# Dealing parts of a weight gradient to fifteen of the sixteen DMA engines, and moving late stores to another queue

## The chip, the cores and the metric

The kernel runs on one core of a Trainium2 chip. The time is what the device needs for one execution, in microseconds; the median of three runs before the change is 733.99 us (733.68 to 734.82).

A core has a matrix engine (PE, with its weight loads PEld), a vector engine (DVE), a scalar engine (ACT), a general one (POOL) and a sequencer for transfers (SP). Transfers between HBM and on-chip memory are issued from the queues of SP, ACT and POOL and carried by 16 DMA engines. In the profile SP's transfers are queue q1, ACT's q10 and Pool's q0.

## The reference

One decode step: forward and backward of `x + attention(layernorm(x)) + mlp(layernorm(x))`, in bf16. One token, model width 640, 32 heads of 128 with caches of 8192 keys and values per head.

```
xn   = layernorm(x)
q    = xn @ wq                               # 640 x 4096
p    = softmax(q k^T * 128**-0.5)            # per head, 8192 keys
o    = p v
out  = x + o @ wo + mlp(xn)                  # wo: 4096 x 640; w1, w3, w2: 640 x 1728 and back
returns out and the gradients of x, k_cache, v_cache, wq, wo, w1, w3, w2
```

Caches and their gradients are 64 MiB each: 128 MiB is read and 128 MiB written for them. wq, wo and their gradients are 5 MiB each. For one token the gradients are outer products: that of V is p times the gradient of o, that of K is the gradient of the scores times q, that of wq is xn times the gradient of q.

## The kernel before

**Per head.** Each head's K and V (2 MiB each) are loaded by SP into three K and two V buffers, up to three heads ahead (`load_k`, `load_v`). `product` multiplies on DVE (line 365) and lets PE sum with an identity matrix (line 367); `row_max`, `exps` and `probs` make the softmax; `attend` and `dscores` make o and the gradient of q on PE. `outer` writes the gradient of V and of K into one of four buffers `ot`, most of it on DVE (line 387), sixteen of 64 rows on ACT (line 380). `store_made` sends a full `ot`, 2 MiB, from ACT's queue (line 403); the last two heads send halves from SP's queue (line 392).

**Per group.** Four heads make a group `g`, eight a batch `b`. A group has 512 columns of wq and a tile `wo_g` of wo. `prep_steps(g + 1)` makes q for the next group from `wq` (line 263), and transposes `wo_g` on PE (line 253) for the gradient of o; these steps run in `gap()`, between the work of a head. `load_wo(g + 1)` is issued from Pool's queue in the second head of a group (line 146), into one of two buffers. `finish_steps(g)` overwrites `wo_g` and the group's wq columns in place with their gradients on ACT (lines 313 and 323) and stores `wo_g` from Pool's queue (line 319).

**wq.** There are two buffers of a batch each, 128 partitions by 5 columns (`ci`) by 1024 elements. Row `5 p + ci` of wq lies in partition `p`, column `ci`: a column of a batch is 128 pieces of 2 KiB, 256 KiB. Batches 0 and 1 are loaded whole by SP. For batches 0 and 1 the gradient goes out from Pool's queue column by column: the first when the batch's second group is finished, then two after each second half of an `outer` (line 396). Batches 2 and 3 are loaded, also by column, into the same buffers from Pool's queue, at places of the third and fourth head of a batch (`WQ_AT`, line 652). A load waits for the store of the column that it overwrites.

**Late stores.** Three stores are put off until head 29: the gradient of wq of batch 2 (1.25 MiB), that of wo of group 6 and that of wq of group 6 (0.625 MiB each). They go out from ACT's queue in one row (`late`, line 697). The last group's wq gradient, `dwq_t`, goes out from ACT's queue at the very end (line 735).

**Order.** Every engine's instructions run in the order in which the program writes them. An instruction that waits holds up all that stands behind it on its engine, and a queue's transfers are issued in the same way.

Of the kernel before, what the change touches and what calls it, by code (L numbers as in the profile page):

```python
# [9 lines left out]
BF16 = mybir.dt.bfloat16  # L10
# [6 lines left out]
P = 128  # L17
# [4 lines left out]
def kernel(  # L22
# [22 lines left out]
    nc = tc.nc  # L45
    H = A_k_cache.shape[1]
    SK = A_k_cache.shape[2]
    DH = A_k_cache.shape[3]
# [3 lines left out]
    NC = D // P  # L52
# [6 lines left out]
    GW = 8  # L59
# [2 lines left out]
    NB = NF + 1  # L62
    ACT_J = 8
    TAIL = 2
    assert H % GW == 0 and GW % GH == 0 and 0 < REST < P and P % GH == 0
    scale = float(DH) ** -0.5

    consts = ctx.enter_context(tc.tile_pool(name="consts", bufs=1))
# [18 lines left out]
    wq_v = A_wq.rearrange("(p ci) n -> p ci n", ci=NC)  # L87
    dwq_v = out_4.rearrange("(p ci) n -> p ci n", ci=NC)
# [9 lines left out]
    with tc.manual_schedule(engines=ORDERED):  # L98
# [22 lines left out]
        grp = {}  # L121
        late = []

        def store(dst, src, later=False):
            if later:
                late.append((dst, src))
            else:
                nc.scalar.dma_start(dst, src)


        wq_bufs = [consts.tile([P, NC, GW * DH], BF16, name=f"wq_{i}") for i in range(2)]

        def load_wq(b, columns=None, queue=None):
            wq_g = wq_bufs[b % 2]
            cols = slice(b * GW * DH, (b + 1) * GW * DH)
            if columns is None:
                nc.sync.dma_start(wq_g[:], wq_v[:, :, cols])
            for ci in columns or ():
                queue.dma_start(wq_g[:, ci, :], wq_v[:, ci, cols])
            for g in range(b * HB, (b + 1) * HB):  # L140
                c0 = (g - b * HB) * GH * DH
                grp.setdefault(g, dict(wq_all=wq_g, wq=wq_g[:, :, c0:c0 + GH * DH]))
# [148 lines left out]
        def on_cols(g):  # L291
            on = small.tile([P, GH], F32, name="on")
            nc.scalar.copy(on[:], grp[g]["on_ps"])
            on_bf = small.tile([P, GH], BF16, name="on_bf")
            nc.scalar.copy(on_bf[:], on[:])
            return on, on_bf
# [8 lines left out]
        def finish_steps(g):  # L305
            G_ = grp[g]
            wo_g = G_["wo"]
            on, on_bf = on_cols(g)
            behind_o.append((g, on_bf))
            yield  # L310
            assert not behind_o
            for r in range(GH):
                nc.scalar.activation(wo_g[:, r, :], g_bc_bf[:], ACTF.Copy, scale=on[:, r:r + 1])
                if r == 1:
                    yield
            if g == NG - 2:
                store(dwo_v[g], wo_g[:], True)
            else:
                nc.gpsimd.dma_start(dwo_v[g], wo_g[:])
            yield  # L320
            b, k = divmod(g, HB)
            for ci in range(NC):
                nc.scalar.activation(G_["wq"][:, ci, :], G_["dqbc"][:].rearrange("p h d -> p (h d)"),
                                     ACTF.Copy, scale=xn_col[:, ci:ci + 1])
            if g < NG - HB and k == HB - 1:
                cols = slice(b * GW * DH, (b + 1) * GW * DH)
                if g == NG - HB - 1:
                    store(dwq_v[:, :, cols], G_["wq_all"][:], True)
                else:
                    columns.extend((dwq_v[:, ci, cols], G_["wq_all"][:, ci, :]) for ci in range(NC))  # L330
                    nc.gpsimd.dma_start(*columns.pop(0))
            if g >= NG - HB:
                store(dwq_v[:, :, g * GH * DH:(g + 1) * GH * DH], G_["wq"], True)
            grp.pop(g)
# [7 lines left out]
        def new_head(h):  # L342
            st = Head()
            st.h = h
            st.g, st.hh = divmod(h, GH)
            st.G = grp[st.g]
            st.K, st.V = kv_tiles.pop(h)
            hs[h] = st
            return st

        def product(st, which, half):
            if which == "S":
                st.q = st.G["qs"][:, st.hh, :]
# [12 lines left out]
            for i in range(DHH // RUN):  # L366
                nc.tensor.matmul(ps[:], lhsT=ident_bf[:], rhs=T[:, :, RUN * i:RUN * (i + 1)],  # L367
                                 start=(half == 0 and i == 0), stop=(half == 1 and i == DHH // RUN - 1))

        def outer(st, vec, w2, wf, dst, h, half):  # L370
            outer_v(st, vec, w2, dst, h, half, outer_s(st, vec, wf, half))
# [12 lines left out]
        def outer_v(st, vec, w2, dst, h, half, j1):  # L384
            j0 = half * JH
            n = j1 - j0
            nc.vector.tensor_tensor(st.ot[:, j0:j1],  # L387
                                    vec.rearrange("p (a b) -> p a b", b=2).unsqueeze(1).to_broadcast([P, n, DH // 2, 2]),
                                    w2[:, j0:j1, :].unsqueeze(2).to_broadcast([P, n, DH // 2, 2]), ALU.mult)
            rows = st.ot[:].rearrange("p j a b -> p j (a b)")  # L390
            if h >= H - TAIL:
                nc.sync.dma_start(dst[h][:, j0:j0 + JH, :], rows[:, j0:j0 + JH, :])
            elif half:
                made.append((dst[h], rows))
                for _ in range(2 if len(columns) > 2 else len(columns)):
                    nc.gpsimd.dma_start(*columns.pop(0))

        columns = []
        made = []

        def store_made():
            while made:
                nc.scalar.dma_start(*made.pop(0))
# [195 lines left out]
        for b in range(NB):  # L599
            rows, src = (P, w2t[:, b, :]) if b < NF else (REST, w2r)  # L600
# [37 lines left out]
        def gap():  # L638
            if steps and next(steps[0], "end") == "end":
                steps.pop(0)  # L640
# [8 lines left out]
        exps(first)  # L649
        product(first, "DP", 1)  # L650
        prev = None
        WQ_AT = {(2, 1): ((0,), nc.gpsimd), (3, 0): ((1,), nc.gpsimd), (3, 1): ((2,), nc.gpsimd), (3, 2): ((3, 4), nc.gpsimd)}

        def wq_columns(h, part):
            b, r = divmod(h, GW)
            if 0 < b < H // GW - 1 and (r, part) in WQ_AT:
                load_wq(b + 1, *WQ_AT[r, part])

        for h in range(H - 1):
            n = new_head(h + 1) if h + 1 < H else None  # L660
            c = hs.pop(h)
            g, hh = divmod(h, GH)
            if n:
                product(n, "S", 0)
            probs(c)
            outer(c, c.do, c.P2, c.Pf, dvc, h, 0)
            if prev:
                keep_dq(prev)
            gap()
            row_dots(c)  # L670
            attend(c)
            turn_wq(c)
            if n:
                product(n, "S", 1)
            outer(c, c.do, c.P2, c.Pf, dvc, h, 1)
            if h + 2 < H:
                load_v(h + 2)
            wq_columns(h, 0)
            if hh == 1 and 0 < g < NG - 1:
                load_wo(g + 1, nc.gpsimd)  # L680
            gap()
            dscores(c)
            store_made()
            outer(c, c.q, c.U2, c.Uf, dkc, h, 0)
            keep_wq(c)
            if n:
                row_max(n)
                product(n, "DP", 0)
            outer(c, c.q, c.U2, c.Uf, dkc, h, 1)
            if h == 0:  # L690
                load_k(4)
            elif 1 < h < H - 3:
                load_k(h + 3)
            wq_columns(h, 1)
            wq_columns(h, 2)
            if h == H - 3:
                for dst, src in late:
                    store(dst, src)
            gap()
            if n:  # L700
                exps(n)
                store_made()
                product(n, "DP", 1)
            weights(c)
            gap()
            if hh == 1 and g + 1 < NG:
                steps.append(prep_steps(g + 1))
            if hh == 2:
                gap()
            prev = c  # L710
# [86 lines left out]
```

## Time and profile before

| | |
|---|---|
| median of three runs | 733.99 us |
| the profiled execution | 733.73 us, its span 732.0 us |
| DVE busy | 630.8 us (86%) |
| PE busy | 550.5 us (75%) |
| ACT busy | 462.1 us (63%) |
| moved by DMA | 303.71 MB, mean 415 GB/s |
| SP's queue (q1) | 153.84 MB, 50.2% of 16 engines' span |
| ACT's queue (q10) | 129.11 MB, 41.6% |
| Pool's queue (q0) | 19.75 MB, 6.5% |

Times inside an execution are microseconds from the start of its span. The page's slices cut the span into 40 equal parts. A window row gives a stretch, its length, the busy time of PE, PEld, DVE, ACT and POOL with the number of instructions, the clock granted to PE, the DMA share (the mean busy share of the 16 DMA engines) and GB/s. A row of the timeline gives start, duration, engine, line and operation; in brackets stands how long the engine had been idle and what ended that. "ACTq" and "SPq" are the queues' own issuing instructions.

### The profile page before, as it was taken

How to read it: one execution, taken by the hardware profiler on the slowest of the kernel's cores; microseconds unless marked ns; L12 is line 12 of the kernel's file. 1: busy time of each engine (PE TensorE's matmuls, PEld its weight loads, DVE VectorE, ACT ScalarE, POOL GpSimd, SP SyncE). 2: the span in 40 equal slices, each digit the busy share in tenths (PEclk: the TensorE clock that was granted, in tenths of full speed). 3: DMA queues.
4: the chain of work that ended last, by engine and by line, in shares of the span. 5: the costliest groups of instructions: out<-in, count | busy, mean ns of one | idle time of the engine just before them, and what ended most of it. 6: DMA issues, size and time to landing. Idle time of an engine off the chain costs nothing.

```text
span 732.0 us, 15729 instructions
## 1 busy us (share of the span) xinstructions
PE 550.5 (75%) x6499; PEld 327.6 (45%) x6513; DVE 630.8 (86%) x720; ACT 462.1 (63%) x1391; POOL 21.9 (3%) x46
## 2 busy tenths in 40 slices
PE   5778887788787648876878674887787878887482
PEld 4654444444444425443444432444444445444151
DVE  4789899999999777988899975999889988999774
ACT  2175656786678464784678743777567846777172
POOL 0010000000001100000000200000000000000000
PEclk9697788868888877887876876877887667777685
DMA  9999999999999999999999999999999999999887
GB/s 360 405 420 427 428 428 424 406 429 428 427 431 427 429 426 428 427 428 429 429 428 428 427 429 429 403 428 428 428 429 422 427 424 428 407 428 421 340 328 281
DMA packets 27687, 303.71 MB, mean 415 GB/s; under 512 B 3084, under 2 KB 4430, under 8 KB 9950
## 3 DMA queue, kind: packets, MB, share of 16 engines
q1 hardware_dynamic: 12914, 153.84, 50.2%
q10 hardware_dynamic: 10764, 129.11, 41.6%
q0 software_dynamic: 3936, 19.75, 6.5%
q8 instruction: 51, 0.84, 0.4%
q14 instruction: 22, 0.18, 0.1%
HBM read 151.34 MB, written 151.34 MB: 414 GB/s over the span
## 4 chain that ended last, share of the span: by engine, by line
DMA 41%; issue 19%; DVE 18%; PE 17%; ACT 4%; SPq 0%; POOL 0%; DVEq 0%; POOLq 0%; ACTq 0%
DMA Kt<-in_A_k_cache_dram 19%; DMA out_dram<-wo_g 9%; DVE T L365 9%; DMA wo_g<-in_A_wo_dram 8%; DVE ot L387 5%; PE psS L367 5%; DMA Vt<-in_A_v_cache_dram 3%; PE psDP L367 3%; ACT ot L380 2%; PE ob L434 2%; PE ob L456 2%; DMA dbc<-in_B_w_dram 2%; DVE DP_sb L441 1%; PE dx_ps L551 1%; PE up_ps L526 1%
## 5 line engine op out<-in xcount | busy, mean ns | idle before, releaser
L367 PEld LDWEIGHTS <-ident_bf 128*128 128x128 bf16 x1024 | 121.1, 120 | 237.2 <-issue 183.0
L367 PE MATMUL psDP<-T,ident_bf 128*128 128x512 bf16 x512 | 178.5, 511 | 58.6 <-DVE T L365 58.6
L365 DVE TENSOR_TENSOR T<-Kt,qs_g 128x4096 bf16<-128x4096 bf16 x64 | 146.5, 2290 | 37.1 <-DMA Kt<-in_A_k_cache_dram 35.3
L380 ACT ACTIVATE ot<-qs_g,Uf 128x128 bf16<-128x128 bf16 x496 | 151.4, 389 | 31.6 <-DVE Uf L454 31.6
L367 PE MATMUL psS<-T,ident_bf 128*128 128x512 bf16 x512 | 149.4, 445 | 27.5 <-DVE T L365 27.4
L380 ACT ACTIVATE ot<-do_g,Pf 128x128 bf16<-128x128 bf16 x504 | 154.0, 389 | 1.0
L365 DVE TENSOR_TENSOR T<-Vt,do_g 128x4096 bf16<-128x4096 bf16 x64 | 146.1, 2283 | 5.0 <-ACT do_g L284 2.8
L387 DVE TENSOR_TENSOR ot<-do_g,P 128x3072 bf16<-128x3072 bf16 (+1 forms) x64 | 112.9, 1763 | 1.1
L387 DVE TENSOR_TENSOR ot<-qs_g,U 128x3072 bf16<-128x3072 bf16 (+1 forms) x64 | 113.2, 1768 | 0.0
L456 PEld LDWEIGHTS <-Kt 128*128 128x128 bf16 x2048 | 58.2, 99 | 11.0 <-issue 7.7
L456 PE MATMUL ob<-U,Kt 128*128 128x1 bf16 x2048 | 57.5, 164 | 1.6 <-DVE U L449 1.5
L434 PEld LDWEIGHTS <-Vt 128*128 128x128 bf16 x2048 | 56.7, 97 | 0.0
L434 PE MATMUL ob<-P,Vt 128*128 128x1 bf16 x2048 | 56.0, 163 | 0.0
L475 ACT ACTIVATE dq_diag<-ident_bf,odq 128x128 bf16<-128x128 bf16 x32 | 12.9, 402 | 67.6 <-DVE odq L471 53.8
L428 ACT ACTIVATE Pf<-E,rZ 128x16 f32<-128x16 f32 x32 | 9.8, 305 | 57.6 <-DVE rZ L424 57.6
L258 ACT COPY woT<-ps_t 128x512 bf16<-128x512 bf16 x40 | 23.1, 579 | 33.3 <-PE ps_t L253 33.2
L253 PE MATMUL ps_t<-ident_bf,wo_g 128*128 128x128 bf16 x160 | 17.8, 242 | 32.0 <-DMA wo_g<-in_A_wo_dram 22.3
L253 PEld LDWEIGHTS <-wo_g 128*128 128x128 bf16 x160 | 13.8, 109 | 42.7 <-DMA wo_g<-in_A_wo_dram 23.8
L407 DVE TENSOR_REDUCE S_sb<-psS 128x64 f32<-128x512 f32 x32 | 22.0, 687 | 5.3 <-PE psS L367 5.3
L419 ACT ACTIVATE E<-S_sb,negM 128x64 f32<-128x64 f32 x32 | 11.1, 346 | 24.0 <-DVE negM L416 23.6
L445 PEld LDWEIGHTS sm<-rdot,ones_fc 128*128 128x128 f32 x64 | 11.2, 197 | 29.7 <-DVE junk L444 26.6
L445 PE MATMUL sm<-rdot,ones_fc 128*128 128x1 f32 x64 | 11.1, 242 | 17.7 <-DVE junk L444 17.6
(158 smaller groups left out, 504.9 us busy)
## 6 DMA issues: line engine op xcount, KB each, us to landing
out_dram<-ot ACTq DMA_DIRECT2D x60, 2048.0 KB, 26.7
Kt<-in_A_k_cache_dram SPq DMA_DIRECT2D x32, 2048.0 KB, 28.1
Vt<-in_A_v_cache_dram SPq DMA_DIRECT2D x32, 2048.0 KB, 22.1
out_dram<-ot SPq DMA_DIRECT2D x8, 1024.0 KB, 8.4
out_dram<-wo_g POOLq DMA_DIRECT2D x6, 640.0 KB, 16.3
wo_g<-in_A_wo_dram POOLq DMA_DIRECT2D x6, 640.0 KB, 16.5
wq<-in_A_wq_dram SPq DMA_DIRECT2D x2, 1280.0 KB, 34.8
out_dram<-wq POOLq DMA_DIRECT2D x10, 256.0 KB, 29.5
```

Source lines behind the costliest of these rows:

```text
L253: nc.tensor.transpose(ps_t[:, hh * DH:(hh + 1) * DH], wo_g[:, hh, ci * P:(ci + 1) * P], ident_bf[:])
L258: nc.scalar.copy(woT[:], ps_t[:])
L365: nc.vector.tensor_tensor(T[:], src[:, :, ds_], vec[:, ds_].unsqueeze(1).to_broadcast([P, J, DHH]), ALU.mult)
L367: nc.tensor.matmul(ps[:], lhsT=ident_bf[:], rhs=T[:, :, RUN * i:RUN * (i + 1)], start=(half == 0 and i == 0), stop=(half == 1 and i == DHH ...
L380: nc.scalar.activation(st.ot[:, j1 - ACT_J + j].rearrange("p a b -> p (a b)"), vec, ACTF.Copy, scale=wf[:, half, j:j + 1])
L387: nc.vector.tensor_tensor(st.ot[:, j0:j1], vec.rearrange("p (a b) -> p a b", b=2).unsqueeze(1).to_broadcast([P, n, DH // 2, 2]), w2[:, j0: ...
L407: nc.vector.tensor_reduce(st.S[:], st.ps["S"][:], AX.X, ALU.add)
L419: nc.scalar.activation(st.E[:], st.S[:], ACTF.Exp, bias=negM[:], scale=1.0, accum_out=rsum[:])
L434: nc.tensor.matmul(st.ob[:, 0:1], lhsT=st.V[:, j, :], rhs=st.P2[:, j, 0:1], start=(j == 0), stop=(j == J - 1), skip_group_check=True)
L445: nc.tensor.matmul(st.sm[:, 4:5], lhsT=ones_f, rhs=rdot[:], start=True, stop=True, skip_group_check=True)
L456: nc.tensor.matmul(st.ob[:, 1:2], lhsT=st.K[:, j, :], rhs=st.U2[:, j, 0:1], start=(j == 0), stop=(j == J - 1), skip_group_check=True)
L475: nc.scalar.activation(dq_diag[:], ident_bf[:], ACTF.Copy, scale=odq[:, 1:2])
```

## The change

Pool's transfers of wq are cut and dealt in a new way. The code keeps a counter `dealt`, modulo 16, of the DMA engine at which it takes the next transfer from Pool's queue to begin when it uses fewer than 16. `sparing(dst, src)` sends a transfer of 128 partitions as two: 120 partitions, to be dealt in 15 shares of 8 partitions, and the last 8 partitions, one to an engine. `turn_lanes(to)` brings the counter to a wanted engine with a small filler, a load of some rows of 2 by 8 elements of wq into a tile that nobody reads: `k` rows move it by `k`, and 17 rows by one. The 120 partitions are always sent with the counter at 5, so that by the code's reckoning they go to engines 5 to 15 and 0 to 3, and not to engine 4.

- The wq gradient of batches 0 and 1 goes out in three parts instead of five: columns 0 and 1, columns 2 and 3 (both by `sparing`), and column 4 as before. The first part goes when the batch's second group is finished, the others one after each second half of an `outer`.
- The loads of batches 2 and 3: columns 0 and 1 in one part by `sparing`, then columns 2, 3 and 4 as before. A part is loaded where single columns were.
- The three late stores and `dwq_t` are issued from Pool's queue instead of ACT's; that of batch 2 goes by `sparing`, all five columns at once. A filler brings the counter back to 0 after them.

In the built program Pool's queue has 60 rows where it had 39 (transfers and its few other instructions), ACT's has four transfers less, and the orders of PE, DVE and SP are as before. On Pool's queue the order at the end of batch 0 is: store of wo, filler of 5 rows, 120 rows, filler of 17, 8 rows, 8 rows, 120 rows, filler of 17, load of wo, store of column 4, and then the loads of batch 2.

```diff
+    LANES = 16
+    SPARED = 4
...
-        def store(dst, src, later=False):
+        def store(dst, src, later=False, by=nc.gpsimd.dma_start):
             if later:
-                late.append((dst, src))
+                late.append((by, dst, src))
             else:
-                nc.scalar.dma_start(dst, src)
+                by(dst, src)
+        lane_pad = consts.tile([P, 2, 2, 8], BF16, name="lane_pad")
+        dealt = [0, 0]
+
+        def turn_lanes(to):
+            k = (to - dealt[0]) % LANES
+            if k:
+                rows = k if k > 1 else LANES + 1
+                nc.gpsimd.dma_start(lane_pad[0:rows, dealt[1] % 2], wq_v[0:rows, 0:2, 0:8])
+                dealt[:] = to % LANES, dealt[1] + 1
+
+        def deal(dst, src, p0, p1):
+            nc.gpsimd.dma_start(dst[p0:p1], src[p0:p1])
+            dealt[0] = (dealt[0] + (LANES - 1 if p0 == 0 else P - p0)) % LANES
+
+        def sparing(dst, src):
+            rows = P - P % (LANES - 1)
+            if dealt[0] == (SPARED + 1 + P - rows) % LANES:
+                deal(dst, src, rows, P)
+                deal(dst, src, 0, rows)
+                turn_lanes(SPARED + 1)
+            else:
+                turn_lanes(SPARED + 1)
+                deal(dst, src, 0, rows)
+                turn_lanes(SPARED + 1)
+                deal(dst, src, rows, P)
...
-        def load_wq(b, columns=None, queue=None):
+        def wq_part(b, c0, n):
+            cols = slice(b * GW * DH, (b + 1) * GW * DH)
+            return wq_bufs[b % 2][:, c0:c0 + n, :], wq_v[:, c0:c0 + n, cols], dwq_v[:, c0:c0 + n, cols]
+
+        def load_wq(b, c0=0, n=NC, by=nc.sync.dma_start):
             wq_g = wq_bufs[b % 2]
-            cols = slice(b * GW * DH, (b + 1) * GW * DH)
-            if columns is None:
-                nc.sync.dma_start(wq_g[:], wq_v[:, :, cols])
-            for ci in columns or ():
-                queue.dma_start(wq_g[:, ci, :], wq_v[:, ci, cols])
+            part, src, _ = wq_part(b, c0, n)
+            by(part, src)
...
                 if g == NG - HB - 1:
-                    store(dwq_v[:, :, cols], G_["wq_all"][:], True)
+                    part, _, dst = wq_part(b, 0, NC)
+                    store(dst, part, True, by=sparing)
                 else:
-                    columns.extend((dwq_v[:, ci, cols], G_["wq_all"][:, ci, :]) for ci in range(NC))
-                    nc.gpsimd.dma_start(*columns.pop(0))
+                    columns.extend((b, *part) for part in WQ_PARTS)
+                    store_columns()
...
                 made.append((dst[h], rows))
-                for _ in range(2 if len(columns) > 2 else len(columns)):
-                    nc.gpsimd.dma_start(*columns.pop(0))
-
+                if columns:
+                    store_columns()
+
+        WQ_PARTS = ((0, 2, True), (2, 2, True), (4, 1, False))
         columns = []
         made = []
+
+        def store_columns():
+            b, c0, n, spare = columns.pop(0)
+            part, _, dst = wq_part(b, c0, n)
+            store(dst, part, by=sparing if spare else nc.gpsimd.dma_start)
...
-        WQ_AT = {(2, 1): ((0,), nc.gpsimd), (3, 0): ((1,), nc.gpsimd), (3, 1): ((2,), nc.gpsimd), (3, 2): ((3, 4), nc.gpsimd)}
+        WQ_AT = {(2, 1): (0, 2, sparing), (3, 0): (2, 1, nc.gpsimd.dma_start), (3, 1): (3, 1, nc.gpsimd.dma_start),
+                 (3, 2): (4, 1, nc.gpsimd.dma_start)}
...
             if h == H - 3:
-                for dst, src in late:
-                    store(dst, src)
+                for by, dst, src in late:
+                    by(dst, src)
+                turn_lanes(0)
```

More of the change, by code (lines that the diff above doesn't have):

```diff
@@ L325, in finish_steps @@
             if g < NG - HB and k == HB - 1:
-                cols = slice(b * GW * DH, (b + 1) * GW * DH)
                 if g == NG - HB - 1:
-                    store(dwq_v[:, :, cols], G_["wq_all"][:], True)
-                else:
-                    columns.extend((dwq_v[:, ci, cols], G_["wq_all"][:, ci, :]) for ci in range(NC))
-                    nc.gpsimd.dma_start(*columns.pop(0))
+                    part, _, dst = wq_part(b, 0, NC)
+                    store(dst, part, True, by=sparing)
+                else:
+                    columns.extend((b, *part) for part in WQ_PARTS)
+                    store_columns()
             if g >= NG - HB:
```

## The prediction

> **What bounds the kernel now.** I read the page's slices first, then the stages by window, the waits, the timelines around the two longest stalls, and last the trace's DMA packets and landings.
>
> ```profile
> DMA  9999999999999999999999999999999999999887
> ...
> 600.00:689.00 89.00, 67.31 (x766) 38.42 (x766) 80.97 (x88) 56.03 (x172) 0.00 (x0) 0.78 1.01 420
> 689.00:694.00 5.00, 0.56 (x9) 0.35 (x9) 2.59 (x2) 0.98 (x4) 0.00 (x0) 0.50 0.38 149
> 694.00:706.00 12.00, 10.68 (x163) 6.73 (x161) 6.67 (x7) 10.00 (x34) 0.00 (x0) 0.78 1.00 411
> 706.00:713.00 7.00, 6.34 (x94) 4.23 (x93) 6.79 (x12) 3.83 (x14) 0.00 (x0) 0.82 0.50 201
> 713.00:726.00 13.00, 4.12 (x97) 3.33 (x96) 9.00 (x21) 4.97 (x11) 0.00 (x0) 0.59 1.00 396
> 726.00:730.00 4.00, 0.00 (x0) 0.00 (x0) 0.00 (x0) 0.00 (x0) 0.00 (x0) 0.50 0.21 69
> ```
>
> The last two numbers of a window row are the DMA share and GB/s. Up to 689 us all 16 DMA engines are busy all the time: the kernel is bound by DMA. After that the share falls to 0.38, then 0.50, then 0.21. One sixteenth is 0.06, and at 691 to 693 and 727 to 730 us the share is 0.08 and 0.09: one engine works alone while fifteen have nothing to do. The trace's landings say the same. Each transfer lands in sixteen parts; in the K load that lands at 682.2 us the fifteenth part is in 8.3 us before the sixteenth. That gap is 0.1 us early on, 2.2 at 237 us, 4.9 at 370, 9.7 at 687. One engine falls ever further behind, and DVE waits for it (35.3 us for Kt in all). In the packets this engine has no idle time from about 20 us to 730: its work sets the end.
>
> Two stalls bear on the change.
>
> ```profile
> 673.75 0.64 ACTq L128 DMA_DIRECT2D out_dram<-wq  x1
> 674.41 0.80 ACTq L128 DMA_DIRECT2D out_dram<-wo_g  x1
> 675.25 0.54 ACTq L128 DMA_DIRECT2D out_dram<-wq  x1
> ...
> 678.78 14.15 ACTq L403 DMA_DIRECT2D out_dram<-ot  x1
> ...
> 692.98 0.40 ACT L475 ACTIVATE dq_diag<-ident_bf,odq 128x128 bf16<-128x128 bf16 x1 [13.82 <-issue]
> ...
> 693.43 0.27 PE L477 MATMUL ps_db<-dq_diag,ones_bf 128*128 128x128 bf16 x1 [10.49 <-ACT dq_diag L475]
> ...
> 697.82 0.36 DVE L449 SCALAR_TENSOR_TENSOR U<-DP_sb,sm,P 128x128 bf16<-128x128 f32 x1 [6.23 <-PE sm L445]
> ```
>
> Behind the three late stores, the next issue on ACT's queue takes 14.15 us where others take 0.34; ACT, then PE, then DVE (6.23 us) stand still.
>
> ```profile
> 232.54 0.55 POOL L331 DMA_DIRECT2D out_dram<-wq  x1 [2.94 <-ACT wq L323]
> 233.16 1.15 POOL L396 DMA_DIRECT2D out_dram<-wq  x2
> ...
> 245.37 0.55 POOL L146 DMA_DIRECT2D wo_g<-in_A_wo_dram  x1 [11.07 <-PE sm L411]
> ...
> 275.44 0.61 PE L253 MATMUL ps_t<-ident_bf,wo_g 128*128 128x128 bf16 x4 [10.01 <-DMA wo_g<-in_A_wo_dram]
> ...
> 278.41 0.29 DVE L416 TENSOR_REDUCE negM<-sm 128x1 f32<-128x128 f32 x1 [7.56 <-PE sm L411]
> ...
> 265.00:275.00 10.00, 0.43 (x2) 0.00 (x0) 5.81 (x5) 4.88 (x16) 0.00 (x0) 0.66 1.01 426
> ```
>
> Here a wo load stands behind three wq parts on Pool's queue, takes 30 us, and PE waits 10 us and DVE 7.6. Yet DMA stays at 1.01: the backlog covers it. The same happens at 449 us (9.75 and 7.29 us).
>
> **The change, part by part.**
>
> *Bytes taken off one engine.* Six parts of 2 columns (four stores, two loads) and the late store of 5 columns are dealt in fifteen shares. An even share is 8 rows of 4 KB, six times, and 8 rows of 10 KB: 272 KB. By the order of Pool's queue in the built program, the 8 left-over rows fall on the spared engine in three parts, 12 KB back. 260 KB at 428 GB/s / 16 = 26.8 GB/s is 9.9 us. The fillers (17 rows of two 16-byte pieces, seven times) put 238 tiny pieces on it: at the 9 ns of the trace's 4-byte packets 2.1 us, at the 48 ns at which 10-byte pieces follow each other in the tail 11.4 us, at least nothing. I take 2.1, since these pieces come between others' large packets. Relief: 7.8 us (-1.5 to 9.9). The other fifteen get 272 KB / 15, 0.7 us each.
>
> *Late stores to Pool's queue.* 2.56 MB leave ACT's queue at 674 us, so the 14.15 us issue should fall to 0.34, and DVE's 6.23 us and the 1.44 us that follow at 701 go (0 to 7.7; I take all, as ACT's other issues show no such time). On Pool's queue these stores wait for ACT's scaling only. Nothing computed stands behind them there.
>
> *What the fifteen gain.* They are idle 0.62 x 5 + 0.50 x 7 = 6.6 us between 689 and 713 and 0.79 x 4 = 3.2 us at the end. The K load of 682.2 us would land with its fifteenth part, near 674 + 0.7 + 6 (the stalls below) = 681. From it to the last DVE product are now 37 us, without the two waits 29.4: done at 710. By DMA the end is later, so late bytes fill the gaps. -6.6 and -3.2, if the relief holds (0 to -9.8). The slow engine, at 732.0 - 7.8 = 724, is then no longer last.
>
> *Pool's queue ahead of the wo load.* It now has four columns ahead of it (1 MB) where it had three, two fillers of 17 rows, one of 5, and the two pieces of 8 rows. Column parts land 5.6 to 6.1 us apart (251.3, 256.9, 263.0); each is four packets and one completion, so about 1.2 us per turn. 120 rows of 2 columns: 10.8; a filler or an empty share: 1.2; 8 rows: 2.6. In sum 1.2 + 10.8 + 1.2 + 2.6 + 1.2 + 10.8 + 1.2 = 29 us, where three columns take 17.7. The wo load lands 11 us later, PE's wait grows from 10 to 21 us and with it DVE's, and behind PE wait SP's next K load (issued at 277.76) and ACT's next store (278.74). What hides it is the backlog: the V load of 263.43 lands on the fifteen at 283 to 286, the ot store of 264.07 at 286 to 290. K's data would now come at about 291. So 0 us if the backlog holds out, 11 if it is gone at once; by these landings 1 to 5 us, I take 3, twice: +6 (0 to 22). DVE itself has room: it idles 50 us between 254 and 683.
>
> *The wq loads* end about 7 us later than 318 us; ps_q of the group that needs them comes one group (four heads of 20.6 us) after the one at 260, about 342: hidden. *The last store, dwq_t,* goes to Pool: issue 0.55 instead of 0.56 us, and SP's stores end later: 0.
>
> Sum against the profiled execution (span 732.0, time 733.73): -3.2 - 6.6 + 0.7 + 6 = -3.1, so 730.6. That run is 0.26 under the median 733.99. The gains have fixed sizes while the 6 is the softest term and leans to less, so I say **730.0**.
>
> **A rule weighed.** The trace has no number of an engine on a packet. What it shows: the lone engine of the last 3 us also carries one of the five packets of the 5-row store at the very end, so it is one of five. The Trainium skill (DMA: Bandwidth & Descriptors, "Why a DMA increments its semaphore by 16 and not by 1") says a 5-row transfer from SP or ACT uses the lowest five engines, which would keep engine 4 possible. The same section says that Pool's transfers take the largest k up to 16 that divides both sides, which gives 15 for 120 rows, but that some direct copies from Pool were seen to give each engine ceil(rows/16): 8 rows to engines 0 to 14 then, and engine 15 would be the spared one. By the one the sum is as above, by the other the relief is nothing and the next rival holds. No run here shows which.
>
> **The rivals.**
>
> *No relief (0.21):* the spared engine isn't the slow one. Against: nothing beyond the five candidates; between one in five and one I choose about 0.75 for the right one. Then the slow engine, never idle, still sets the end: 12 KB and the fillers add 0.5 to 2.5, and stalls cost it little, as it is 2 to 8 us behind: 734 to 737, about 735.
>
> *The wo load starves DMA (slower, 0.15):* place: 265 to 292 and 439 to 466 us. Each microsecond in which the fifteen find no issued transfer is paid. It decides once the two stalls cost over 9 us together; at 9 each the sum is 733.73 - 9.1 + 18 = 743. For it: SP's and ACT's issues do stand behind PE. Against: 20 us of transfers are issued when the stall begins.
>
> *Fillers sent piece by piece (0.04):* 34 turns of 1.4 us on one engine, 47 us each, two of them ahead of each wo load: over 800. Against: on Pool's queue 2-KB rows go in 4-KB packets and 1,280-byte rows in 5,120.
>
> *All of the backlog holds (0.07):* no cost at the wo loads: 724.6 by the fifteen, 724 to 726 in all.
>
> **How the numbers follow.** The likeliest, 0.53, lies at 726 to 733. A run can tell about 0.2%, 1.5 us, from no change. Faster (under 732.5): 0.50 of the likeliest and 0.07 of the full gain, with 0.02 of the others: 0.59. Same: 0.03 + 0.08 of no relief + 0.02: 0.13. Slower: 0.28. Range 723 to 740: below lies little, above half of the starving case and the fillers, together under 2 in 10.
>
> **What would show it.** Right: the ot issue at about 675 takes 0.34 us and DVE's wait of 6.23 us is gone; fifteenth and sixteenth part of late K loads land within 3 us; the DMA share stays near 1 from 690 to the end and no lone engine is left. PE's wait for wo_g at 275 grows to about 21 us with the DMA share there at 0.85 or more. Wrong: the lag between fifteenth and sixteenth part grows as before (no relief); a DMA share under 0.7 for over 10 us near 285 or 460 (starving); wo loads of 80 us (fillers).

## The result, and the profile after

The changed kernel takes 741.79 us (median of 5 runs, 738.62 to 742.61) where the kernel before takes 733.97 (5 runs, 733.09 to 734.82). The ratio is 1.0100, with a 95% interval of 1.0075 to 1.0125: it is 1% slower, where 730.0 was predicted. Its profiled execution took 738.62 us, its span 736.7; it is the fastest of the five, so what the other four lost beyond it is not in the profile.

First the slices of its page, which answer to the one row shown of before.

```profile
DMA  8999999999999999999999999999999999999997
GB/s 360 411 419 427 431 427 427 423 430 426 428 428 427 422 402 349 332 431 427 430 428 426 430 418 406 351 353 427 429 430 427 430 428 424 430 429 426 430 421 293
```

The DMA share says the engines were busy throughout, and of the dip at the end of before (887) only the last slice's 7 is left. GB/s says something else: it falls to 349 and 332 near 280 to 310 us, and to 351 and 353 near 465 to 500. The windows show what happens there, and at the end (length, busy PE, PEld, DVE, ACT, POOL with counts, clock, DMA share, GB/s).

```profile
250.00:280.00 30.00, 11.22 (x112) 6.10 (x111) 17.56 (x19) 11.68 (x38) 4.12 (x6) 0.73 1.01 409
280.00:286.00 6.00, 0.00 (x0) 0.00 (x0) 0.00 (x0) 0.00 (x0) 1.16 (x2) 0.50 0.96 408
286.00:292.00 6.00, 3.45 (x72) 2.96 (x73) 0.48 (x2) 0.74 (x2) 0.54 (x1) 0.50 0.89 245
292.00:298.00 6.00, 5.76 (x34) 2.79 (x34) 5.26 (x7) 1.60 (x6) 0.00 (x0) 0.80 1.03 342
298.00:304.00 6.00, 4.91 (x89) 3.53 (x89) 5.96 (x6) 5.97 (x20) 0.00 (x0) 1.00 0.90 377
304.00:312.00 8.00, 5.95 (x87) 3.50 (x84) 7.54 (x10) 6.49 (x20) 0.00 (x0) 1.00 0.91 287
312.00:320.00 8.00, 6.41 (x37) 2.90 (x38) 7.79 (x11) 4.90 (x20) 0.00 (x0) 0.79 1.00 428
...
690.00:700.00 10.00, 5.53 (x66) 3.01 (x65) 6.58 (x9) 4.69 (x17) 0.00 (x0) 0.98 1.01 428
700.00:713.00 13.00, 10.98 (x125) 6.14 (x123) 12.75 (x16) 7.86 (x27) 0.00 (x0) 0.74 1.00 422
713.00:726.00 13.00, 7.29 (x178) 5.98 (x176) 12.08 (x24) 7.33 (x20) 0.84 (x1) 0.68 1.01 421
```

The end is as predicted: 428 and 422 GB/s in 690 to 713 us, where before had holes of 149 and 201. At 280 to 286 us PE, DVE and ACT do nothing, and the transfers that had been issued still keep DMA at 408 GB/s. At 286 the issued loads and `ot` stores run out. Only packets of Pool's queue are left, and they are slow (those of 4 KB take 242 ns on the mean, where 159 is usual): 245 GB/s at a share of 0.89, a hole. Then follows what the prediction had no term for: compute is back, yet for 20 us more DMA moves 287 to 377 GB/s, at a share of 0.90 to 1.03.

The waits (total, times, longest) and the timeline (start, duration, queue, line, operation) name the cause.

```profile
PE ps_t L283 <- DMA wo_g<-in_A_wo_dram: 59.6, 6, 24.0
...
DVE negM L452 <- PE sm L447: 44.1, 3, 21.6
...
DVE T L395 <- DMA Kt<-in_A_k_cache_dram: 11.8, 4, 3.2
```

```profile
236.55 1.86 POOL L144 DMA_DIRECT2D out_dram<-wq  x3
249.71 0.95 POOL L140 DMA_DIRECT2D lane_pad<-in_A_wq_dram  x1 [11.31 <-DMA lane_pad<-in_A_wq_dram]
250.66 0.60 POOL L176 DMA_DIRECT2D wo_g<-in_A_wo_dram  x1
...
263.13 0.33 SPq L119 DMA_DIRECT2D Vt<-in_A_v_cache_dram  x1
290.88 0.33 SPq L112 DMA_DIRECT2D Kt<-in_A_k_cache_dram  x1
...
680.60 0.34 ACTq L439 DMA_DIRECT2D out_dram<-ot  x1
```

The wo load is issued at 250.66 and lands at 288.5 us; PE waits 23.4 us for it, and 24.0 at the second such place. SP issues nothing for 27.8 us (263.13 to 290.88). The wait of DVE for Kt fell from 35.3 to 11.8 us, and ACT's issue of an `ot` store takes 0.34 us where one took 14.15. In the landings the sixteenth part of a K load comes 0 to 1.5 us after the fifteenth from 300 us on, where it had come 3 to 10 us after.

What a stretch costs DMA is worked out from a window row: its length, less its bytes at 428 GB/s, the rate of the full stretches. The kernel before has 427 GB/s in 250 to 320 us, 421 in 440 to 500 and 311 from 680 to its end at 732: 0.2, 1.0 and 14.2 us lost. Its rows, and behind them those of the changed kernel:

```profile
250.00:320.00 70.00, 49.00 (x588) 28.63 (x589) 56.14 (x61) 42.17 (x130) 3.28 (x6) 0.80 1.01 427
440.00:500.00 60.00, 43.10 (x502) 25.20 (x503) 48.98 (x53) 40.11 (x119) 1.63 (x3) 0.77 1.01 421
680.00:732.00 52.00, 24.37 (x365) 15.94 (x363) 32.69 (x50) 19.79 (x62) 0.00 (x0) 0.70 0.77 311
...
250.00:320.00 70.00, 37.70 (x426) 21.79 (x427) 44.59 (x51) 31.38 (x101) 5.82 (x9) 0.76 0.98 374
440.00:500.00 60.00, 31.03 (x411) 19.07 (x409) 36.95 (x41) 27.55 (x87) 2.64 (x4) 0.74 0.97 373
680.00:736.70 56.70, 31.08 (x441) 19.36 (x439) 41.59 (x59) 25.81 (x81) 0.84 (x1) 0.71 0.91 382
```

That is 54/428 of 70 = 8.8 us, 7.7 us and 6.1 us. The two stalls cost 15.3 us more than before, the end 8.1 us less. With some 2.4 us less lost elsewhere that makes the 4.9 us by which this execution is longer (738.62 against 733.73).

### The profile page after: what moved, and what is told of

Its sections match the earlier page's. It is cut to its first block, busy times and chain, and to the rows that moved or that the text cites. A ratio compares the mean times of both kernels' runs of the same rounds, so it can differ in the third digit from the quotient of the medians.

```text
span 736.7 us, 15743 instructions
## 1 busy us (share of the span) xinstructions
PE 542.4 (74%) x6497; PEld 323.0 (44%) x6513; DVE 630.4 (86%) x720; ACT 462.0 (63%) x1391; POOL 35.3 (5%) x60
## 5 line engine op out<-in xcount | busy, mean ns | idle before, releaser
L397 PEld LDWEIGHTS <-ident_bf 128*128 128x128 bf16 x1024 | 119.3, 119 | 221.1 <-issue 165.5
L397 PE MATMUL psDP<-T,ident_bf 128*128 128x512 bf16 x512 | 173.9, 501 | 53.4 <-DVE T L395 53.4
L395 DVE TENSOR_TENSOR T<-Kt,qs_g 128x4096 bf16<-128x4096 bf16 x64 | 146.5, 2289 | 19.8 <-DMA Kt<-in_A_k_cache_dram 11.8
L397 PE MATMUL psS<-T,ident_bf 128*128 128x512 bf16 x512 | 146.7, 439 | 18.2 <-DVE T L395 18.2
L452 DVE TENSOR_REDUCE negM<-sm 128x1 f32<-128x128 f32 x32 | 9.1, 284 | 44.1 <-PE sm L447 44.1
```

## The experiments

**Theory at the start:** the whole loss is made at the two wo loads that stand behind a longer Pool queue. **Rivals:** the small pieces and fillers cost DMA time wherever they are; the gain at the end comes of the moved stores, and not of leaving out engine 4.

### One part behind the wo load

```diff
-                if columns:
+                if columns and dst is dkc:
                     store_columns()
```

> The changed kernel, with the second wq part of a batch sent behind the wo load instead of ahead of it; the bytes, the pieces and the fillers stay. Theory (the loss of the change is made at the two wo loads that stand behind a longer Pool queue): one part of 120 rows and one of 8 less ahead of the load, so PE's longest wait for wo_g falls from 24 to about 10 to 13 us, the 15 us that the DMA engines lose in 250 to 320 and 440 to 500 us fall to under 4, and the time is 725 to 729 us. Rival (the small pieces and fillers themselves slow the DMA engines, wherever they stand): PE's wait falls but the lost time stays, 738 to 742 us.

729.64 us (10 runs, 726.99 to 737.79), ratio 0.9954 (0.9924 to 0.9985). Moving one part of two columns, twice in the kernel, takes 12.1 us off the changed kernel, and the result is 0.5% faster than before; it lies 0.6 us above the range of the theory and far below that of the rival. The execution under the profile was the longest of the ten and no good picture of it, so the kernel was run twice more.

> A second look at the run with one part behind the wo load, whose profiled execution was the longest of its ten (737.8 against a median of 729.6 us) and showed the sixteenth part 5 to 10 us behind from 400 us on. Theory (an execution in which the engine left out is not the one that lags, as others are): an execution near 729 us shows the sixteenth part within 3 us of the fifteenth all through, one above 734 us shows the lag. Rival (the lag has nothing to do with it): a lag at 729 us too, or none at 735 us.

One time, 735.10 us, with the sixteenth part 0 to 5 us late up to 660 us and up to 8 after. A long execution with the lag is what the theory had; one execution decides little.

> The run with one part behind the wo load once more, timed in five rounds. Theory (its profiled executions fell on its long side by chance): a median of 728 to 731 us, a spread of 10 us, and a profiled execution anywhere in it. Rival (its profiled executions are longer by themselves): the same median, the profiled execution again 4 us or more above it.

729.78 us (6 runs, 727.91 to 732.43), the execution under the profile 730.90: anywhere in the spread, as this theory had it. What makes the spread of 10 us, and why the lag differs from one execution to the next (about 3 us at 690 us in this one, 7 to 11 in the longest), stays open. Here PE's waits for wo_g at the two places are 11.7 and 12.5 us, and DMA loses 1.6 and 2.0 us there and 9.1 at the end.

### All parts behind the wo load

```diff
-                    store_columns()
...
-                if columns:
+                if columns and (dst is dkc or h % GW == 2):
```

> As the run before, with all wq parts of a batch behind the wo load. Theory (stalls at the wo loads): no wait of PE for wo_g over 3 us, no time lost there, 723 to 727 us, 0 to 3 us below the run with one part ahead; the wq loads come one or two parts later, and if PE then waits for them near 340 us, some of it is given back. Rival (pieces and fillers): 736 to 742 us.

A miss: 737.67 us (10 runs), ratio 1.0045 (1.0020 to 1.0071), in the rival's range. But the time is not lost where the pieces are (1.4 us in 250 to 320 us, 2.2 in 440 to 500). The timeline shows where the stall went.

```profile
315.02 0.54 POOL L349 DMA_DIRECT2D out_dram<-wo_g  x1 [7.45 <-ACT wo_g L343]
352.76 0.53 POOL L176 DMA_DIRECT2D wo_g<-in_A_wo_dram  x1 [37.20 <-DMA out_dram<-wo_g]
...
369.27 0.61 PE L283 MATMUL ps_t<-ident_bf,wo_g 128*128 128x128 bf16 x4 [14.44 <-DMA wo_g<-in_A_wo_dram]
```

The later parts push the wq loads back, and behind those stands the next group's store of wo, which takes 37 us to land. The next wo load overwrites its buffer and waits for it. PE's wait is now 14.4 us up to 369 us, and 17.9 up to about 549; by the same reckoning 4.5 us are lost in 320 to 440 us and 8.8 in 500 to 680.

### The wo load from SP's queue

```diff
+            if hh == 0 and 0 < g < NG - 1:
+                load_wo(g + 1, nc.sync)
```

after `load_k`, in place of the load from Pool's queue in the second head; once on the changed kernel, once on the kernel before.

> The changed kernel with the load of wo issued from SP's queue, behind the K load of a group's first head, instead of from Pool's; the parts, the fillers and their order stay. Theory (the loss is made by the wo load standing behind the longer Pool queue): PE waits for wo_g under 3 us, no time lost in 250 to 320 and 440 to 500 us, and of the changed kernel's 741.8 us some 15 go: 724 to 729 us. Rival (putting the wq parts on the queue that way costs DMA time by itself, and only moves from place to place, as it did with all parts behind the wo load): 734 us or more, with stalls somewhere else.

> The kernel before with the same move of the wo load to SP's queue. Its own waits for wo_g (10 and 9.75 us) go. Theory (DMA was never idle behind these waits, and the lagging engine sets the end): 731.5 to 734.5 us, within 2 us of before. Rival (these waits cost before time as well, so the gain of the move is the move's and not that of the change): 725 to 730 us.

739.96 us (6 runs), ratio 1.0073 (1.0054 to 1.0092), and on the kernel before 735.91 (11 runs), ratio 1.0027 (1.0015 to 1.0040). On the changed kernel the time is in the range of the rival, which also had stalls somewhere else; on the kernel before neither had it. PE's waits are gone (2.7 us at most), but the edit makes a wait of its own:

```profile
252.80 0.33 SPq L176 DMA_DIRECT2D wo_g<-in_A_wo_dram  x1
253.23 1.52 SPq L119 DMA_DIRECT2D Vt<-in_A_v_cache_dram  x1
254.84 1.51 SPq L112 DMA_DIRECT2D Kt<-in_A_k_cache_dram  x1
```

```profile
DVE T L395 <- DMA Vt<-in_A_v_cache_dram: 43.9, 6, 11.7
```

SP waits until 252.8 us for the store of the wo buffer, with the next V and K loads queued behind that wait, and DVE then waits 43.9 us for Vt (32.5 in the edit of the kernel before). So these two runs say nothing for or against the theory; they show that a transfer with a wait costs what stands behind it on its queue.

### Late stores alone, and another engine left out

```diff
                 for dst, src in late:
-                    store(dst, src)
+                    nc.gpsimd.dma_start(dst, src)
```

on the kernel before, and `SPARED = 9` in the run with one part behind the wo load.

> The kernel before, with its three late stores issued whole from Pool's queue; nothing is dealt to fifteen engines. Theory (two separate gains: ACT's 14 us issue, and the relief of the engine that lags): the issue falls to under 1 us and DVE's 6.2 us wait behind it goes, but the lag of the sixteenth part stays at 8 to 10 us and the lone engine sets the end: 732 to 735 us. Rival (the gain at the end is that of the queue alone): 725 to 729 us, and the lone engine's stretch is gone without any sparing.

> The run with one part ahead of the wo load, with engine 9 left out instead of engine 4. Theory (engine 4 is the one that lags, and the counter names it rightly): the lag of the sixteenth part grows as in the kernel before, and a little more, to 9 to 12 us at 687 us, and a lone engine works at the end: 733 to 738 us. Rival (any sparing does, or the gain comes of the queues and the order alone): as with engine 4 left out, 725 to 729 us, with a lag under 3 us.

In time both came as the theory had it. Late stores alone: 733.37 us (10 runs), ratio 0.9992 (0.9980 to 1.0004), not to be told from no change; ACT's long issue is gone, yet the sixteenth part is 8 to 13 us late at 680 to 710 us. Engine 9 left out: 737.19 us (5 runs), ratio 1.0043 (1.0028 to 1.0057), 7.5 us slower than with engine 4, the sixteenth part 4 to 7 us late at 640 to 700 us (9 to 12 were expected near 687) and up to 10 after. By the code's counter engine 4 is the one that lags; leaving it out rather than engine 9 is worth 7.5 us in this order of the queue. No third engine was tried.

### Whole parts

```diff
         def sparing(dst, src):
+            nc.gpsimd.dma_start(dst, src)
+            return
```

> The changed kernel with each part sent whole, over sixteen engines, and no filler: the same columns at the same places, no small piece. Theory (what stands ahead of the wo load is mostly the bytes of four columns): PE's longest wait for wo_g is 17 to 22 us, and at 4 to 7 us lost at each of the two places, with the lagging engine at the end as before, the time is 738 to 746 us. Rival (the fillers and pieces make the stall, by their turns and completions): a wait of 12 to 15 us, a loss under 2 us each, 732 to 736 us.

```profile
PE ps_t L285 <- DMA wo_g<-in_A_wo_dram: 32.7, 4, 13.8
```

734.92 us (10 runs), ratio 1.0007 (0.9993 to 1.0021): the rival, but for 3.1 us lost at the second place, where it had under 2. With the same four columns ahead of the wo load, PE waits 13.8 and 12.3 us; dealing them makes it 23.4 and 24.0. So ten of the 24 us come of the dealing itself. The trace's packets show how, by their starts on Pool's queue ahead of the first wo load. A part of two columns takes about as long dealt as whole: 248.7 to 258.8 and 266.0 to 277.8 us dealt, 243.8 to 254.5 and 254.7 to 265.5 whole. While the 120 packets of 4 KB of a dealt part go out, eight lone packets of 8 bytes follow each other, most of them 1.2 us apart (250.1 to 258.1 and 267.1 to 275.9 us); with whole parts there are none. The trace does not name the engine; by their number and place these are the empty share of the engine that is left out, which takes as many turns as a share with rows. What whole parts do not have is the time between: the fillers and the pieces of 8 rows take 246.3 to 248.7, 258.8 to 266.0 and 277.8 to 280.2 us, 12.0 in all for three fillers and two pieces. That is 2.4 us each, by estimate two turns of 1.2 us: one for their small packet, one for the 4-byte packet that follows it.

### The stall without any dealing

```diff
-                for _ in range(2 if len(columns) > 2 else len(columns)):
+                for _ in range(len(columns)):
                     nc.gpsimd.dma_start(*columns.pop(0))
```

on the kernel before: five whole columns ahead of the wo load.

> The kernel before with all five columns of a batch's wq gradient ahead of the wo load on Pool's queue instead of three, whole and by column: a long wait for wo_g as in the changed kernel, without pieces, fillers or an engine left out. Theory (each stall costs DMA time of its own): PE's longest waits for wo_g are 18 to 24 us, 4 to 8 us are lost in each of 250 to 320 and 440 to 500 us; nothing else gives it back: 740 to 748 us. Rival (a stall lets the lagging engine catch up, so the end gets shorter by what the stall cost): the same loss at the two places, but the lag of the sixteenth part under 3 us after 300 us, the stretch after 680 us without a lone engine, and 733 to 738 us.

741.82 us (4 runs, 739.86 to 743.38), ratio 1.0106 (1.0086 to 1.0127). A stall alone makes the time of the whole change. PE's longest waits are 21.4 and 25.1 us.

```profile
285.00:290.00 5.00, 1.80 (x55) 1.80 (x56) 0.00 (x0) 0.59 (x1) 0.00 (x0) 0.50 0.63 257
290.00:296.00 6.00, 6.00 (x43) 3.12 (x41) 4.39 (x5) 1.62 (x5) 0.00 (x0) 0.68 0.83 248
296.00:302.00 6.00, 4.67 (x49) 2.83 (x49) 5.82 (x9) 4.62 (x14) 0.00 (x0) 1.00 0.99 415
302.00:308.00 6.00, 6.00 (x112) 3.82 (x109) 4.64 (x6) 3.04 (x9) 0.00 (x0) 0.72 0.76 265
...
689.00:700.00 11.00, 2.25 (x10) 0.80 (x8) 9.12 (x9) 0.77 (x3) 0.00 (x0) 0.66 0.99 414
```

The same hole and a slow stretch behind it, with no piece in the kernel. Pool's 4-KB packets take 160 ns here, and engines without any packet make up more of the losses than in the changed kernel, 4.1 and 4.6 us. And a surprise at the end: 414 GB/s at 689 to 700 us, though no engine is left out and ACT's long issue is still there (12.93 us at 686). The sixteenth part is at most 2.6 us late from 290 us on: a stall in which DMA empties lets the lagging engine catch up.

```profile
250.00:320.00 70.00, 40.58 (x414) 22.57 (x414) 43.32 (x48) 30.59 (x96) 2.73 (x5) 0.71 0.94 380
440.00:500.00 60.00, 29.85 (x369) 17.57 (x368) 35.81 (x40) 26.34 (x84) 1.64 (x3) 0.72 0.92 370
680.00:738.10 58.10, 31.25 (x440) 19.50 (x438) 40.03 (x56) 25.03 (x80) 0.00 (x0) 0.65 0.91 371
```

Lost: 7.9 and 8.1 us at the stalls, 14.8 more than before; 7.7 at the end, 6.5 less. Both theories are half right: the stalls cost what the first had, and part of it comes back at the end, as the rival had it, but less than half.

### The changed kernel with engine 9 left out

```diff
-    SPARED = 4
+    SPARED = 9
```

> The changed kernel with engine 9 left out in place of engine 4; every part stands where the change put it, and the long waits for wo_g stay. Theory (leaving out engine 4 is what brings the sixteenth part back, worth some 8 us): the lag grows on after 300 us, to 4 us or more at 687 us, a lone engine works at the end, and the time is 746 to 751 us. Rival (the two stalls, in which the DMA engines run empty, bring the lag back, whichever engine is left out): a lag under 2 us all through and 740 to 743 us.

745.27 us (4 runs), ratio 1.0156 (1.0140 to 1.0171): between the two. Engine 4 is worth 3.5 us beside the stalls and 7.5 without them, since the stalls bring part of the lag back by themselves (from 300 to 660 us it is at most 2.4 us).

### Dealing less

```diff
-        WQ_PARTS = ((0, 2, True), (2, 2, True), (4, 1, False))
+        WQ_PARTS = ((0, 1, False), (1, 2, False), (3, 2, False))
...
-        WQ_AT = {(2, 1): (0, 2, sparing), (3, 0): (2, 1, nc.gpsimd.dma_start), (3, 1): (3, 1, nc.gpsimd.dma_start),
+        WQ_AT = {(2, 1): (0, 2, nc.gpsimd.dma_start), (3, 0): (2, 1, nc.gpsimd.dma_start), (3, 1): (3, 1, nc.gpsimd.dma_start),
```

The first pair of lines sends the stores of batches 0 and 1 whole, with three columns ahead of the wo load as in the kernel before; the second run has both pairs and loads batches 2 and 3 whole too.

> The changed kernel with the wq gradient of batches 0 and 1 sent whole, with one and two columns ahead of the wo load as in the kernel before; the loads of batches 2 and 3 and the late store of batch 2 are still dealt to fifteen engines. Theory (relief by bytes left off engine 4, no long stall): about 140 KB less on it, 5 us, PE's longest wait for wo_g 10 to 13 us: 728 to 731 us. Rival (pieces cost wherever they are): 733 to 737 us.

> As the run before, with the loads of batches 2 and 3 whole as well: only the late store of batch 2 is dealt to fifteen engines, with a filler on either side. Theory (relief by bytes): 80 KB, 3 us: 730 to 732 us, a lag as in the kernel before up to 660 us and 3 us less after. Rival (no relief, as the late stores whole on Pool's queue gave none): 733 to 735 us.

730.75 us (4 runs), ratio 0.9956 (0.9941 to 0.9971); 732.40 (10 runs), ratio 0.9982 (0.9972 to 0.9993): the first as the theory had it, the second 0.4 us above its range. With the late store alone dealt, the lag of the K and V loads goes from 6 to 7 us at 600 to 625 us to under 1 at 640 to 680, that of the `ot` stores from about 10 to between 5.6 and 6.3. By bytes, 80 KB at 26.8 GB/s, 3.0 us were to come back in that one transfer; it is 3.5 us and more. PE's waits are 8.0 to 11.2 us in these two, and 0.6 us or less is lost at each place.

### A stall beside the relief, and one more part dealt

```diff
-                if columns:
+                while columns:
                     store_columns()
```

on the run with whole stores; and there, `(3, 2, True)` for the last part, which goes behind the wo load.

> The run with the stores of batches 0 and 1 whole (730.75 us), with all five columns ahead of the wo load: the long stall beside the relief that the dealt loads and the dealt late store give, and no piece ahead of a wo load. If a stall and the relief add: 730.75 + 7.9 = 738.6, so 738 to 739.5 us. If a stall brings the lag back by itself and leaves the relief nothing to give: 741 to 743 us, as with five columns alone, with a lag under 2.5 us from 300 us on.

> The run with the stores of batches 0 and 1 whole, with the last two columns of each, behind the wo load, dealt to fifteen engines again: 64 KB more off engine 4, 2.4 us. Theory (relief by bytes, where no long stall is made): 728 to 730 us. Rival (the pieces cost what the relief gives): 730.5 to 733 us.

The stall beside the relief: 736.41 us (10 runs), ratio 1.0027 (1.0012 to 1.0043). That is below both expectations, and 5.7 us more than without the stall. It does not decide between the two, for the stall is shorter than with five columns alone: PE's waits are 19.9 and 19.5 us, the losses 5.2 and 4.8, 10.0 together against 16.0. In the profiled execution (732.74 us, the fastest of the ten) stall and relief do not simply add: against the run with whole stores 9.1 us more are lost at the two places and 3.8 less from 680 us on, and the sixteenth part of the K, V and `ot` transfers is at most 2.7 us late from 300 us on. One more part dealt: 728.83 us (6 runs, 727.67 to 732.35), ratio 0.9941 (0.9920 to 0.9962), the lowest median of all; its difference to the two runs of 729.6 and 729.8 is within their spread.

## Why the prediction was wrong

| kernel | PE's two waits, us | lost there, us | lost from 680 us on | median, us |
|---|---|---|---|---|
| before | 10.0, 9.7 | 0.2, 1.0 | 14.2 | 733.97 |
| whole stores | 8.3, 8.4 | 0.3, 0.6 | 9.3 | 730.75 |
| whole parts | 13.8, 12.3 | 0.8, 3.1 | 14.6 | 734.92 |
| one part behind, timed | 11.7, 12.5 | 1.6, 2.0 | 9.1 | 729.78 |
| whole stores, five columns ahead | 19.9, 19.5 | 5.2, 4.8 | 5.5 | 736.41 |
| five columns, nothing dealt | 21.4, 25.1 | 7.9, 8.1 | 7.7 | 741.82 |
| the change | 23.4, 24.0 | 8.8, 7.7 | 6.1 | 741.79 |

(Losses from the window rows of one execution each.) Up to a wait of some 10 us the issued transfers cover it. At 12 to 14 us 1 to 3 us are lost, at 20 us 5, at 21 to 25 us 8 to 9.

**What failed: "+6" for Pool's queue ahead of the wo load.** The step took 3 us at each place, "0 us if the backlog holds out, 11 if it is gone at once". Measured: 8.8 and 7.7 us, 15.3 more than before together; by the medians, the order of the two-column part alone is 12.1 us (741.79 against 729.64). The wait itself was nearly right, 21 us predicted and 23.4 and 24.0 measured. (DVE idles 57 us between 254 and 683 us before, not the 50 that the step names; nothing hangs on it.) So was the cover: the issued V load and `ot` store were done at 286 to 290 us. The hole itself cost no more than was taken for it. What the step left out is what follows.

```profile
286.00:292.00 6.00, 3.45 (x72) 2.96 (x73) 0.48 (x2) 0.74 (x2) 0.54 (x1) 0.50 0.89 245
292.00:312.00 20.00, 16.61 (x206) 9.83 (x205) 18.76 (x21) 14.06 (x43) 0.00 (x0) 0.94 0.94 330
463.00:469.00 6.00, 2.92 (x71) 2.82 (x72) 0.00 (x0) 0.58 (x1) 0.54 (x1) 0.50 0.97 317
469.00:488.00 19.00, 15.86 (x203) 9.59 (x202) 17.73 (x20) 12.70 (x38) 0.00 (x0) 0.92 0.94 324
```

By these rows 2.6 and 1.6 us are lost in the hole, and 4.6 and 4.6 in the 20 and 19 us behind it, the refill. The rest, about 1.6 us at either place, is for the most part lost ahead of the hole, while the dealt parts are under way and packets of Pool's queue and `ot` stores slow down; the step held that the small pieces "come between others' large packets". In the refill, after the queues have run empty, loads and stores come one after the other instead of together, and in the trace's packets the loads are slow while they are alone: 16 KB take 878 and 877 ns on the mean in the first 3 us (292 to 295 and 469 to 472 us) and 858 at 304 to 312 us, where 611 is usual. By kind, slow load packets make up 3.4 us of the loss at either place, slow packets of Pool's queue 2.9 and 2.1, slow `ot` stores 0.7 and 0.5, and engines without any packet only 1.7 and 1.6. The end of a stall was priced as the moment at which transfers are issued again; it is the moment at which both directions run again, some 20 us later. The step's own bounds, 0 to 11 us a place, held; its choice of 3 did not.

**The rival that came true** is "the wo load starves DMA", at its two stalls and nearly at its price: 9 us a stall, 743 us. It had 0.15. That the price came so near is in part luck: the rival pays for the time in which the engines find no issued transfer, and that is under a fifth of the loss at the first place and about a fifth at the second; the rest is slow packets, and half of the loss and more lies behind the places that it names (265 to 292 and 439 to 466 us). The sign named for it, a DMA share under 0.7 for over 10 us, did not come: the share stayed at 0.89 to 1.03, because a slow packet counts as busy. GB/s showed it. Nearly all the signs named for a right forecast came as well (0.34 us for the `ot` issue, a lag of 2 us at most from 300 us on, a wait of 23.4 us at a share of 0.85 or more), so they could not tell the two apart.

**Bytes taken off one engine:** right in kind. It is engine 4, by the code's counter (7.5 us between leaving out 4 and 9), so the rival of no relief falls. The rule that was weighed can be decided too: by the Trainium skill (DMA: Bandwidth & Descriptors, "Why a DMA increments its semaphore by 16 and not by 1") 120 rows go in 15 shares, and these runs agree (engine 9 in place of engine 4 costs 7.5 us); by the exception named there, with engine 15 spared, 4 and 9 would have been alike. In size the relief was too high where no stall helps: 260 KB were to give 7.8 us of lag and the gains of 6.6 and 3.2 us, and dealing 208 to 272 KB gave 4.1 to 5.1 us against before, with 9.1 and 11.7 us still lost after 680 us in the profiled executions of the one part behind (timed) and of the last part dealt. Where DMA empties, the lag comes back by itself, and 6.5 of the 8.1 us gained at the end of the changed kernel also came with five columns and no dealing. The terms of the sum were not independent.

**Late stores to Pool's queue:** ACT's issue takes 0.34 us and DVE's 6.23 us wait is gone, as predicted; alone it gains 0.6 us, within what can't be told from nothing, as the lagging engine then still sets the end.

**Fillers:** not piece by piece on one engine at 47 us each (17 rows go as one packet of 544 bytes), but the small transfers cost more than was counted. The step had 10.8 us for 120 rows of two columns, measured 10.1 and 11.8; and 7.4 us for three fillers, the pieces of 8 rows and an empty share, measured 12.0. Dealing lengthened PE's wait by 10 to 12 us (23.4 and 24.0 against 13.8 and 12.3).

By terms: the gains of 9.1 us came out at about 6.7 in the kernel with one part behind the wo load, of which 2.4 go at its own two waits of 12 us (4.3 net by the medians). The stalls, put at 6, came to these 2.4 and 12.1 more, the difference of the two medians: 733.97 - 6.7 + 14.5 = 741.8. This split leans on that one run; beside the stalls the gains and the lag change as well.

## What to carry to other kernels

Price a stall of a DMA-bound kernel in two parts: what the issued transfers don't cover, and the refill, until loads and stores run together again; here the first was 2.6 and 1.6 us, the second 4.6 at either place. Watch GB/s beside the DMA share, for slow packets look busy. Before bytes are moved within a queue, look for the one transfer behind them that a compute engine waits for, and keep it in front, without pushing back what others wait for: the change makes the kernel 1% slower, and 0.5% faster with two columns of batches 0 and 1 moved behind the wo load; with all columns behind it, the stall only moved.

## What the runs showed of the hardware

- A 16-KB load packet takes 611 ns beside stores, and 878 and 934 on the mean in the 3 us after its queue had run empty with no store beside it (292 to 295 and 304 to 307 us; 287 GB/s in the row of 304 to 312). Stores alone at 301 to 304 us keep their rate (38.5 ns per KB against 38.2). It is not loads alone as such: in the page's second slice, 18 to 37 us, when nothing but loads is in flight, the rate is 411 GB/s. What slows them after an empty stretch was not settled. The Trainium skill (DMA: Bandwidth & Descriptors, "Latency and other measured facts") reports lower rates for copies whose rows lie a large power of two apart in HBM, at pitches of 512 KiB and more, and calls the mechanism, streams in lock step, an inference. The rows of these loads lie 16 KiB apart, which it does not cover, and no run here tests it.
- While a dealt transfer of 2-KB pieces is under way, its own 4-KB packets take up to 1.4 us where 159 ns is usual, and stores of other queues slow down too: 46 ns per KB on the mean, where 38.2 is usual, at 602 to 618 us in the run with the wo load on SP's queue, with few loads beside them. Over a whole run the mean of the 4-KB packets is 163 ns with the parts sent whole and 168 to 193 with parts dealt. When almost nothing but Pool's packets was left, it was 242 ns in the changed kernel (286 to 292 us) and 160 with five columns and nothing dealt (282 to 292 us). Why was not tried.
- An engine that gets no row of a transfer still takes turns for it, as read from the number and place of 8-byte packets: eight of 9 ns, 1.2 us apart, beside the eight 4-KB packets of each other engine as long as other queues are full, and in a burst when they are empty (287 to 289 us).
- The lag of one engine is no fixed debt: two stretches in which DMA ran empty held it at 2.6 us or less for the rest of the kernel, with nothing taken off that engine.
